# Attention and Silu FFN on one core: output weights by column halves, shorter segments, decay tables moved to GpSimd

## The chip, the core and the metric

The kernel runs on one core of a Trainium2 chip. The core has a matrix engine (TensorE, PE in the profile, its weight loads PEld), three engines for elementwise work (VectorE or DVE, ScalarE or ACT, GpSimd or POOL), and SyncE (SP), which here only issues transfers. Engines run on their own and wait for each other through semaphores. Matrix results land in PSUM and must be copied out ("evicted") by VectorE or ScalarE. Transfers between HBM and the on-chip SBUF are issued by SyncE or GpSimd and carried by 16 DMA engines.

The metric is device time in microseconds (us), the median of the timed executions.

## The reference

Four sequences of 768 positions, eight heads of 64. A linear attention with decay runs over blocks of 64 positions and carries a 64x64 state per head; its output goes through a two-layer FFN with Silu.

```python
for b in range(nb):                       # nb = 12 blocks
    qb, kb, vb = (q[:, :, sl], k[:, :, sl], v[:, :, sl])
    intra = np.einsum('bhic,bhjc->bhij', qb, kb) * Dmask[None]
    intra = np.einsum('bhij,bhjd->bhid', intra, vb)
    inter = np.einsum('bhid,bhde->bhie', qb * lam_pow[None], kv_state)
    out[:, :, sl] = intra + inter
    kb_dec = kb * rev_pow[None]
    kv_state = lam_block[None, :, None, None] * kv_state + np.einsum('bhsd,bhse->bhde', kb_dec, vb)
# ... x = out, heads side by side: 3072 x 512
h = x @ w_in                              # 512 x 2048
g = h * (1.0 / (1.0 + np.exp(-h)))        # Silu
return (g @ w_out)                        # 2048 x 512, result 3072 x 512
```

## The kernel before

Everything is written as small operations with priorities. A planner inside the kernel, which runs while the program is built, gives each a place on an engine. The order on every engine is fixed by that; at run time only semaphores decide when an operation starts.

The 3072 rows are 24 chunks of 128 (two blocks each). Chunks are gathered into groups for the FFN. The names in the profile: `h` is a PSUM tile of FFN1 (also used for transposes), `g` its Silu, `o` the PSUM tile of FFN2, `ob` the result. `big` is a pool of three 1 MB staging buffers, shared by w_in, w_out and v.

```python
GROUPS = [2, 2, 2, 2, 2, 2, 4, 4, 4]      # chunks in each FFN group
NHALF = 0                                 # groups whose FFN2 runs in two column halves
VP = 3                                    # the first VP segments have v issued by SyncE, the others by GpSimd
ORDER = "k0 q0 v0 k1 v1 wi0 wi1 q2 k2 v2 k3 v3 wi2 wi3 G:v3 S0 wo0 wo1 wo2 wo3 G:wo2 S1 S2 S3 S4 S5 S6"
SEGS = [(0, 8, 4), (1, 0, 4), (1, 4, 8), (2, 0, 6), (2, 6, 6), (3, 0, 6), (3, 6, 6)]   # sequence, first block, blocks
```

ORDER is the order in which loads are issued: k, q and v of the first four chunks, w_in and w_out in four pieces each, then segments S0 to S6, which bring k, q and v of the other chunks. `G:v3` is a gate: GpSimd waits there until v3 has landed. A segment's k comes in eight transfers (one per head) from GpSimd, cast on the way; its v in eight transfers as well.

A weight piece is loaded into `big` and cast to bf16 in two halves, by VectorE or ScalarE:

```python
def load_w(which, i, cast=False):
    if which == "in":
        src, dst = w_in_r[:, :, 512 * i:512 * i + 512], w_in_bf[:, :, 512 * i:512 * i + 512]
    else:
        src, dst = w_out_r[:, 4 * i:4 * i + 4, :], w_out_bf[:, 4 * i:4 * i + 4, :]
    # ... (a casting load, unused here)
    nc.sync.dma_start(out=t.tile, in_=src)                  # t: a buffer of big
    # ... for j in range(2): d, r are halves of dst and t.tile
        nc.scalar.activation(d, r, AF.Copy)                 # or
        nc.vector.tensor_copy(d, r)
        # ... wdep[which, m] = this cast, for the row blocks m that it brings
```

The FFN of a group. FFN2 sums over 16 row blocks of w_out, so the last of its matmuls needs the last piece:

```python
def ffn1(g, m0):
    # ...
            for ko in range(4):
                nc.tensor.matmul(hb.tile[:, i, :], lhsT=w_in_bf[:, ko, m * 128:(m + 1) * 128], rhs=xt[g].tile[:, ko, :], ...)
    # ...
        nc.scalar.activation(gb.tile, hb.tile..., AF.Silu)

def ffn2(g, mt):
    parts = 2 if g < NHALF else 1
    w = DM // parts
    for part in range(parts):
        # ...
        for kk in range(4):
            # ... for m in range(4 * kk, 4 * kk + 4):
                    nc.tensor.matmul(po.tile, lhsT=gt.tile[...], rhs=w_out_bf[:, m, cs], start=(m == 0), stop=(m == 15))
            deps += [wdep["out", m] for m in ms]
        # ... eviction of po to ob by VectorE or ScalarE, then two output transfers
```

The decay factors of the positions are six tables in `tabo`. The first is an exponential; the other five are the first times a power of lambda per head pair, made by ScalarE in four operations each. VectorE multiplies the attention's output by its table to give x. The buffers that hold k of a segment are zeroed by VectorE before their first use:

```python
zk = [const.tile([128, 8, NP, 2, D], BF16, name=f"kseg{i}") for i in range(3)]
o_zk = [[add(lambda t=t, i=i: nc.vector.memset(t[:, i], 0.0), ("DVE", 280.0), prio=-20.0 + 5.0 * n) for i in range(8)]
        for n, t in enumerate(zk)]
# ...
for i in range(1, NB):                    # NB = 6
    o_tabs.append([add(lambda i=i, p=p: nc.scalar.activation(
        tabo[:, p, i * C:i * C + C], tabo[:, p, 0:C], AF.Copy, scale=tab[:, 76 + 4 * i + p:77 + 4 * i + p]),
        ("ACT", 300.0), prio=TPR[i], at=TAT[i], deps=o_tabs[0]) for p in range(NP)])
```

ScalarE holds the tables of its functions in sets, and a set must be loaded before a function of it runs. The kernel asks for the set with exponential and logarithm at its start; the load for Silu is placed ahead of the first Silu. While TensorE has nothing to do in the first 26 us of the plan, it multiplies zeros (`zt`, L845).

Of the kernel before, what the change touches and what calls it, by code (L numbers as in the profile page):

```python
# [7 lines left out]
F32 = mybir.dt.float32  # L8
BF16 = mybir.dt.bfloat16
# [3 lines left out]

GROUPS = [2, 2, 2, 2, 2, 2, 4, 4, 4]
NHEAD = 4
NHALF = 0
NPET = 12
NPETQ = 16
WARM = 26000.0
VP = 3  # L20
ORDER = "k0 q0 v0 k1 v1 wi0 wi1 q2 k2 v2 k3 v3 wi2 wi3 G:v3 S0 wo0 wo1 wo2 wo3 G:wo2 S1 S2 S3 S4 S5 S6"
SEGS = [(0, 8, 4), (1, 0, 4), (1, 4, 8), (2, 0, 6), (2, 6, 6), (3, 0, 6), (3, 6, 6)]


class Op:
# [23 lines left out]
LATE = 60000.0  # L49
BIAS = 100.0  # L50
BIAS2 = 0.0
ZP = [[-150.0, -65.0, -64.0], [-140.0, -63.0, -50.0], -61.5]
TAT = [0.0, 10000.0, 17000.0, 19000.0, 30000.0, 31000.0]
TPR = [-90.0, -44.0, -43.0, -42.0, -22.0, -21.0]


# [114 lines left out]
def kernel(  # L171
# [20 lines left out]
    psum = ctx.enter_context(tc.tile_pool(name="psum", bufs=1, space=bass.MemoryType.PSUM))  # L192
    ctx.enter_context(tc.manual_schedule())

    SLOTS = {"qf": 3, "qb": 3, "qT": 4, "big": 3, "kbh": 2, "kfh": 2, "vfh": 3, "kseg": 3, "kT": 4, "vs": 3, "vbd": 3,
             "ss": 3, "sbd": 3, "x": 3, "g": 24, "ob": 5, "sc": 1, "op": 1, "kv": 1, "h": 3, "o": 2}
    PS = {"sc", "op", "kv", "h", "o"}

# [37 lines left out]


    zkh = [const.tile([128, 2, NP, 2, D], BF16, name=f"kbh{i}") for i in range(SLOTS["kbh"])]
    zk = [const.tile([128, 8, NP, 2, D], BF16, name=f"kseg{i}") for i in range(SLOTS["kseg"])]
    zv = [const.tile([128, 2, NP, 2, D], BF16, name=f"vbd{i}") for i in range(SLOTS["vbd"])]  # L240
    zs = [const.tile([128, NP, 2, D], BF16, name=f"sbd{i}") for i in range(SLOTS["sbd"])]
    nc.vector.memset(zkh[0], 0.0)
# [84 lines left out]
    def load_kh(c, eng, cast=False):  # L327
        if cast:
            t, os = Buf("kbh"), []
            r = k[0, :, C * c:C * c + C, :].rearrange("(p two) (s t) d -> two t s p d", two=2, t=2)  # L330
            for h in range(2):
                for s in range(2):
                    def f(h=h, s=s):
                        t.tile = zkh[t.idx % SLOTS["kbh"]]
                        hs = slice(64 * h, 64 * h + 64)
                        nc.gpsimd.dma_start(out=t.tile[hs, s, :, h, :], in_=r[h, s])
                    os.append(load(f, 65536, 128.0, 256, eng="POOL", alloc=[] if os else [t], uses=[t] if os else []))
            return t, os, None, None
        t, tf = Buf("kbh"), Buf("kfh")
        r = k[0, :, C * c:C * c + C, :].rearrange("(p two) (s t) d -> two s p (t d)", two=2, t=2)  # L340
        os = []
        for h in range(2):
            hs = slice(64 * h, 64 * h + 64)

            def f(h=h, hs=hs):
                if h == 0:
                    new(tf, [128, NP, 2, D], F32)
                QS[eng].dma_start(out=tf.tile[hs].rearrange("a p s d -> a p (s d)"), in_=r[h])
            o = load(f, 131072, 225.0, 256, eng=eng, alloc=[] if h else [tf], uses=[tf] if h else [])

            def fc(e, h=h, hs=hs):
                if h == 0:
                    t.tile = zkh[t.idx % SLOTS["kbh"]]
                dst, src = t.tile[hs, :, :, h], tf.tile[hs].rearrange("a p s d -> a s p d")
                if e == "ACT":
                    nc.scalar.activation(dst, src, AF.Copy)
                else:
                    nc.vector.tensor_copy(dst, src)
            os.append(add(fc, [("DVE", 420.0), ("ACT", 500.0)], deps=[o], alloc=[] if h else [t],
                          uses=[tf] + ([t] if h else []), after=os[-1:], prio=c - 62))  # L360
            if t.idx < 2 and h == 0:
                os[-1].deps += o_zkh[t.idx]
        return t, os, tf, o
# [14 lines left out]
    def load_kseg(b, c0, n):  # L378
        t = Buf("kseg")
        os = []  # L380
        for hh in range(H):
            def f(hh=hh):
                p, two = divmod(hh, 2)
                t.tile = zk[t.idx % SLOTS["kseg"]]
                hs = slice(64 * two, 64 * two + 64)
                nc.gpsimd.dma_start(out=t.tile[hs, 0:n, p, two, :],  # L386
                                    in_=k[b, hh, 64 * c0:64 * (c0 + n), :].rearrange("(c s) d -> s c d", s=64))
            os.append(load(f, 16384 * n, 128.0, 64 * n, eng="POOL", alloc=[] if hh else [t], uses=[t] if hh else [],
                           deps=o_zk[t.idx] if t.idx < SLOTS["kseg"] else []))
        return t, os  # L390

    def load_vseg(b, c0, n, eng):
# [12 lines left out]

    wdep, wlast = {}, {}

    def load_w(which, i, cast=False):

        if which == "in":  # L410
            src, dst = w_in_r[:, :, 512 * i:512 * i + 512], w_in_bf[:, :, 512 * i:512 * i + 512]
        else:
            src, dst = w_out_r[:, 4 * i:4 * i + 4, :], w_out_bf[:, 4 * i:4 * i + 4, :]
        if cast:
            o = load(lambda: nc.gpsimd.dma_start(out=dst, in_=src), 1048576, 312.0, 512, eng="POOL")
            for m in range(4 * i, 4 * i + 4):
                wdep[which, m] = o
            return

        t = Buf("big")  # L420

        def f():
            new(t, [128, 4, 512], F32)
            nc.sync.dma_start(out=t.tile, in_=src)
        o = load(f, 1048576, 370.0, 512, alloc=[t], issue=450.0)
        wlast[which, i] = (t, o)
        for j in range(2):
            def fc(e, j=j):
                if which == "in":
                    d, r = dst[:, :, 256 * j:256 * j + 256], t.tile[:, :, 256 * j:256 * j + 256]  # L430
                else:
                    d, r = dst[:, 2 * j:2 * j + 2, :], t.tile[:, 2 * j:2 * j + 2, :]
                if e == "ACT":
                    nc.scalar.activation(d, r, AF.Copy)  # L434
                else:
                    nc.vector.tensor_copy(d, r)
            z = add(fc, [("DVE", 750.0), ("ACT", act_ns(1024, True))], deps=[o], uses=[t], prio=-20 + 0.1 * i)
            for m in range(4 * i + 2 * j, 4 * i + 2 * j + 2):
                wdep[which, m] = z

    gt_ = const.tile([128, 16], F32, name="gt_")
    ngate = [0]
# [284 lines left out]
    def ffn2(g, mt):  # L727
# [4 lines left out]
        for part in range(parts):  # L732
# [3 lines left out]
            for kk in range(4):  # L736
                ms = range(4 * kk, 4 * kk + 4)

                def f(kk=kk, ms=ms, po=po, cs=cs):
                    if kk == 0:  # L740
                        new(po, [128, w], F32, padded=[128, DM])
                    for m in ms:
                        gt, _, g0 = gts[g, m]
                        nc.tensor.matmul(po.tile, lhsT=gt.tile[:, g0 + mt * C:g0 + (mt + 1) * C], rhs=w_out_bf[:, m, cs],  # L744
                                         start=(m == 0), stop=(m == 15))
                deps = [gts[g, m][1] for m in ms] + ([prev] if prev else [])
                deps += [wdep["out", m] for m in ms]
                prev = add(f, ("PE", pe_ns(4, w)), deps=deps, alloc=[po] if kk == 0 else [],
                           uses=([] if kk == 0 else [po]) + list({id(gts[g, m][0]): gts[g, m][0] for m in ms}.values()),
                           prio=PF + 100 * g + 20 + 4 * mt + kk + (8 if part else 0))  # L750
# [20 lines left out]
    def zero(t, cols, first, prio):  # L771
        if first:
# [5 lines left out]
    o_zs = [zero(t, 512, i == 0, ZP[0][i]) for i, t in enumerate(zs)]  # L778
    o_zv = [zero(t, 1024, i < 2, ZP[1][i]) for i, t in enumerate(zv)]
    o_zkh = [[], zero(zkh[1], 1024, True, ZP[2])]  # L780
    o_zk = [[add(lambda t=t, i=i: nc.vector.memset(t[:, i], 0.0), ("DVE", 280.0), prio=-20.0 + 5.0 * n) for i in range(8)]
            for n, t in enumerate(zk)]
    o_iota = add(c_iota, ("POOL", 1000.0), prio=-200)
    chain["POOL"].append(o_iota)
    o_id = add(c_ident, ("DVE", 300.0), prio=-199, deps=[o_iota])
# [2 lines left out]
    o_tab = add(c_tab, ("ACT", 1700.0), at=3400.0, prio=-100, deps=[o_id])  # L788
    o_tabs = [[add(lambda p=p: nc.scalar.activation(tabo[:, p, 0:C], io, AF.Exp, scale=lla[:, p:p + 1]), ("ACT", 300.0),
                   prio=-90, deps=[o_tab]) for p in range(NP)]]  # L790
    for i in range(1, NB):
        o_tabs.append([add(lambda i=i, p=p: nc.scalar.activation(  # L792
            tabo[:, p, i * C:i * C + C], tabo[:, p, 0:C], AF.Copy, scale=tab[:, 76 + 4 * i + p:77 + 4 * i + p]),
            ("ACT", 300.0), prio=TPR[i], at=TAT[i], deps=o_tabs[0]) for p in range(NP)])

    def seg(i):
        b, c0, n = SEGS[i]
# [9 lines left out]
    for item in ORDER.split():  # L807
# [8 lines left out]
        elif item[0] == "q":  # L816
            landed[item] = load_q(int(item[1]), "POOL" if item[2:] == "p" else "SP")
        elif item[0] == "w":
            which = "in" if item[1] == "i" else "out"
            load_w(which, int(item[2]), item[3:] == "c")  # L820
            landed[item] = wlast.get((which, int(item[2])))
        elif item[0] == "S":
            seg(int(item[1]))
        else:
            buf, dep = landed[item[2:]]
            gate(buf, dep)
# [56 lines left out]
```

## Time and profile before

| | |
|---|---|
| time, median of 3 | 226.24 us (225.97 to 226.25) |
| span of the profiled execution | 225.2 us |
| TensorE busy | 212.4 us (94%), 1898 matmuls |
| ScalarE busy | 124.9 us (55%) |
| VectorE busy | 108.5 us (48%) |
| GpSimd busy | 68.9 us (31%) |
| warm-up matmuls on zt | 82 |
| HBM read, written | 27.27 MB, 6.29 MB |

The page's second part cuts the span into 40 slices of 5.6 us and gives the busy tenths of each engine in each; its row PEclk is the clock granted to TensorE. The table of stages gives busy time between two points in time. The chain of waits goes back from the last instruction, at each step to what released it; a line is a start, a length and the work. A busy TensorE need not be doing useful work, and matmuls overlap: the mean duration of one is longer than the distance from one to the next, so prices are taken from runs of equal matmuls in the chain.

### The profile page before, as it was taken

What the parts mean: (1) busy time and instruction counts of PE and PEld (TensorE: products, weight loads), DVE (VectorE), ACT (ScalarE), POOL (GpSimd) and SP (SyncE); (2) the same over time, 40 slices, a digit from 0 to 9 for tenths busy, and PEclk for the clock granted to TensorE, in tenths of its full rate; (3) what the DMA queues carried; (4) which work ended last, traced back from release to release, by engine and by line L of the source; (5) the groups of instructions that cost most, each with busy time, mean ns of one, the idle gap of its engine ahead of it and who ended that gap; (6) DMA issues with size and microseconds to landing.
All of it is one profiled execution on the core that took longest, in us unless ns stands there. A gap on an engine that the chain in (4) does not pass through costs nothing.

```text
span 225.2 us, 4817 instructions
## 1 busy us (share of the span) xinstructions
PE 212.4 (94%) x1898; PEld 136.6 (61%) x1922; DVE 108.5 (48%) x244; ACT 124.9 (55%) x236; POOL 68.9 (31%) x111
## 2 busy tenths in 40 slices
PE   6996999799999999999999999999999999999991
PEld 4785888666488487879578554555455444444440
DVE  7987696364476527897358255363644100000000
ACT  6799899765185276556338346741375512555211
POOL 2000910086635499887736470000000000000000
PEclk9999699999999999999999999999999999999999
DMA  4999999689999988999999999395220013300052
GB/s 126 264 361 234 374 191 345 214 260 194 228 215 272 160 194 178 159 194 222 205 129 237 156 173 163 92 153 107 67 50 0 3 29 76 82 0 3 0 125 62
DMA packets 64485, 35.44 MB, mean 157 GB/s; under 512 B 48848, under 2 KB 54992, under 8 KB 64464
## 3 DMA queue, kind: packets, MB, share of 16 engines
q1 hardware_dynamic: 39968, 24.13, 49.7%
q0 software_dynamic: 24352, 11.02, 34.8%
q8 instruction: 15, 0.25, 0.5%
q14 instruction: 6, 0.05, 0.1%
q10 hardware_dynamic: 144, 0.00, 0.0%
HBM read 27.27 MB, written 6.29 MB: 149 GB/s over the span
## 4 chain that ended last, share of the span: by engine, by line
PE 80%; ACT 12%; DMA 4%; issue 1%; SPq 1%; DVE 1%; ACTq 0%
PE o L744 34%; PE h L712 34%; PE op L644 4%; DMA qf<-in_q_dram 2%; ACT w_in_bf L434 2%; PE h L516 2%; ACT g L720 2%; PE kv L664 2%; PE sc L616 2%; ACT tabo L792 2%; ACT sbd L676 1%; PE h L480 1%; ACT vbd L559 1%; DMA out_dram<-ob 1%; ACT w_out_bf L434 1%
## 5 line engine op out<-in xcount | busy, mean ns | idle before, releaser
L712 PE MATMUL h<-x,w_in_bf 128*128 128x256 bf16 (+1 forms) x569 | 90.5, 309 | 1.4 <-ACT w_in_bf L434 0.5
L744 PE MATMUL o<-w_out_bf,g 128*128 128x512 bf16 x367 | 86.3, 379 | 2.3 <-ACT w_out_bf L434 1.4
L720 ACT ACTIVATE g<-h 128x512 bf16<-128x512 f32 x96 | 57.2, 597 | 30.2 <-PE h L712 29.7
L712 PEld LDWEIGHTS <-w_in_bf 128*128 128x128 bf16 x576 | 54.7, 99 | 27.2 <-ACT w_in_bf L434 1.4
L744 PEld LDWEIGHTS <-g 128*128 128x128 bf16 x384 | 36.0, 98 | 39.8 <-issue 1.7
L386 POOL DMA_DIRECT2D kseg<-in_k_dram x56 | 37.3, 690 | 18.4 <-DMA qf<-in_q_dram 14.6
L756 ACT ACTIVATE ob<-o 128x512 f32<-128x512 f32 x24 | 14.3, 598 | 49.5 <-PE o L744 38.6
L678 DVE CAST sbd<-kv 64x256 bf16<-64x256 f32 x40 | 16.9, 421 | 20.5 <-PE kv L664 16.6
L401 POOL DMA_DIRECT2D big<-in_v_dram x32 | 21.1, 671 | 8.3 <-DMA kseg<-in_k_dram 4.6
L691 DVE TENSOR_TENSOR x<-op,tabo 128x512 bf16<-128x512 f32 x24 | 16.5, 689 | 9.7 <-PE op L644 8.7
L676 ACT ACTIVATE sbd<-kv 64x256 bf16<-64x256 f32 x40 | 15.0, 376 | 10.6 <-PE kv L664 10.1
L622 DVE TENSOR_TENSOR ss<-sc,mask 128x512 bf16<-128x512 f32 x20 | 13.8, 688 | 11.6 <-PE sc L616 11.6
L644 PE MATMUL op<-ss,vbd 128*128 128x64 bf16 (+1 forms) x192 | 16.3, 197 | 0.0
L644 PE MATMUL op<-qT,sbd 128*128 128x64 bf16 (+1 forms) x160 | 15.0, 195 | 0.0
L845 PE MATMUL sc<-zt 128*128 128x256 bf16 x82 | 13.6, 318 | 1.1 <-DVE zt L228 1.1
L561 DVE COPY vbd<-vs 64x512 bf16<-64x512 bf16 x44 | 14.0, 318 | 0.5
L644 PEld LDWEIGHTS <-vbd 128*128 128x128 bf16 x192 | 12.6, 98 | 1.7 <-ACT vbd L559 0.3
L550 DVE TENSOR_TENSOR vs<-big,tab 128x512 bf16<-128x512 f32 x20 | 13.1, 685 | 0.9 <-DMA big<-in_v_dram 0.8
L523 DVE COPY kT<-h 128x1024 bf16<-128x1024 bf16 x9 | 6.0, 686 | 14.6 <-PE h L516 14.6
L644 PEld LDWEIGHTS <-sbd 128*128 128x128 bf16 x160 | 11.6, 98 | 1.4
L845 PEld LDWEIGHTS <-zt 128*128 128x128 bf16 x82 | 8.9, 114 | 2.7 <-DVE zt L228 1.1
L310 POOL DMA_DIRECT2D qf<-in_q_dram x10 | 9.1, 912 | 4.4 <-ACT g L720 1.7
(58 smaller groups left out, 144.7 us busy)
## 6 DMA issues: line engine op xcount, KB each, us to landing
out_dram<-ob SPq DMA_DIRECT2D x48, 128.0 KB, 3.4
qf<-in_q_dram POOLq DMA_DIRECT2D x10, 512.0 KB, 8.4
big<-in_moe_w_in_dram SPq DMA_DIRECT2D x4, 1024.0 KB, 7.8
big<-in_moe_w_out_dram SPq DMA_DIRECT2D x4, 1024.0 KB, 6.2
big<-in_v_dram POOLq DMA_DIRECT2D x32, 96.0 KB, 5.9
kseg<-in_k_dram POOLq DMA_DIRECT2D x32, 48.0 KB, 7.0
kfh<-in_k_dram SPq DMA_DIRECT2D x8, 128.0 KB, 5.4
qf<-in_q_dram SPq DMA_DIRECT2D x2, 512.0 KB, 8.2
```

What stands on the lines that cost most here:

```text
L386: nc.gpsimd.dma_start(out=t.tile[hs, 0:n, p, two, :], in_=k[b, hh, 64 * c0:64 * (c0 + n), :].rearrange("(c s) d -> s c d", s=64))
L401: QS[eng].dma_start(out=t.tile[hs, :, p, :], in_=v[b, hh, 64 * c0:64 * (c0 + n), :].rearrange("(c s) d -> s c d", s=64))
L561: nc.vector.tensor_copy(vb.tile[hs, :, :, h, :], tv.tile[hs])
L644: nc.tensor.matmul(o_cols(p, sub), lhsT=l, rhs=r, start=not ovs["started"], stop=i == len(steps) - 1, skip_group_check=True)
L676: nc.scalar.activation(nb.tile[hs, :, h, :], kvp.tile[hs], AF.Copy)
L678: nc.vector.tensor_copy(nb.tile[hs, :, h, :], kvp.tile[hs])
L691: nc.vector.tensor_tensor(xt[g].tile[:, :, C * off:C * off + C], ob.tile, tabo[:, :, C * blk:C * blk + C], op=AL.mult)
L712: nc.tensor.matmul(hb.tile[:, i, :], lhsT=w_in_bf[:, ko, m * 128:(m + 1) * 128], rhs=xt[g].tile[:, ko, :], start=(ko == 0), stop=(ko == 3) ...
L720: nc.scalar.activation(gb.tile, hb.tile.rearrange("a i n -> a (i n)"), AF.Silu)
L744: nc.tensor.matmul(po.tile, lhsT=gt.tile[:, g0 + mt * C:g0 + (mt + 1) * C], rhs=w_out_bf[:, m, cs], start=(m == 0), stop=(m == 15))
L756: nc.scalar.activation(bo.tile[:, cs], po.tile, AF.Copy)
L845: nc.tensor.matmul(zp, lhsT=zt[:, 0:128], rhs=zt, start=nz == 0, stop=True, skip_group_check=True)
```

## The change

Four things are changed together.

- w_out is loaded in pieces of eight row blocks by 256 columns instead of four row blocks by 512. The first two groups compute FFN2 in column halves (NHALF = 2), so that the left half needs only the first two pieces. The order of the loads is changed to bring these ahead of the first segment S0, which is gated by the third piece of w_in.
- All segments are of four blocks; there are ten instead of seven, with five smaller buffers for k instead of three. Only the first segment's v is issued by SyncE.
- The tables 2 to 5 are made by GpSimd, one operation each; table 1 stays on ScalarE. The zeroing of the later k buffers is put off.
- Silu's table set is asked for right after the first decay table.

They are meant to let the FFN start earlier and to relieve ScalarE and VectorE at the start.

```diff
-NHALF = 0
+NHALF = 2
-VP = 3
-ORDER = "k0 q0 v0 k1 v1 wi0 wi1 q2 k2 v2 k3 v3 wi2 wi3 G:v3 S0 wo0 wo1 wo2 wo3 G:wo2 S1 S2 S3 S4 S5 S6"
-SEGS = [(0, 8, 4), (1, 0, 4), (1, 4, 8), (2, 0, 6), (2, 6, 6), (3, 0, 6), (3, 6, 6)]
+VP = 1
+ORDER = "k0 q0 v0 k1 v1 wi0 wi1 q2 k2 v2 k3 v3 wi2 wi3 wo0 wo1 G:wi2 S0 wo2 wo3 G:wo2 S1 S2 S3 S4 S5 S6 S7 S8 S9"
+SEGS = [(0, 8, 4)] + [(b, c, 4) for b in range(1, 4) for c in (0, 4, 8)]
...
+TPOOL = (2, 3, 4, 5)
+ZAT = [0.0, 34000.0, 38000.0, 45000.0, 50000.0, 55000.0]
-TAT = [0.0, 10000.0, 17000.0, 19000.0, 30000.0, 31000.0]
+TAT = [0.0, 10000.0, 0.0, 0.0, 0.0, 0.0]
...                                        # SLOTS: kseg 3 -> 5
-    zk = [const.tile([128, 8, NP, 2, D], BF16, name=f"kseg{i}") ...
+    zk = [const.tile([128, 4, NP, 2, D], BF16, name=f"kseg{i}") ...
...                                        # load_w
-            src, dst = w_out_r[:, 4 * i:4 * i + 4, :], w_out_bf[:, 4 * i:4 * i + 4, :]
+            r0, cs = 8 * (i % 2), slice(256 * (i // 2), 256 * (i // 2) + 256)
+            src, dst = w_out_r[:, r0:r0 + 8, cs], w_out_bf[:, r0:r0 + 8, cs]
...                                        # ffn2
-                deps += [wdep["out", m] for m in ms]
+                deps += [wdep["out", m, hf] for m in ms for hf in ((part,) if parts == 2 else (0, 1))]
...
-    o_zk = [[add(lambda t=t, i=i: nc.vector.memset(t[:, i], 0.0), ..., prio=-20.0 + 5.0 * n) for i in range(8)]
+    o_zk = [[add(lambda t=t, i=i: nc.vector.memset(t[:, i], 0.0), ..., prio=-20.0 + 5.0 * n, at=ZAT[n])
+             for i in range(4)] for n, t in enumerate(zk)]
...
+    add(lambda: nc.scalar.preload_act_table_set("silu_and_others"), ("ACT", 1290.0), prio=-89, after=o_tabs[0])
+
+    def scaled(i, p=None):
+        if p is None:
+            nc.gpsimd.tensor_tensor(tabo[:, :, i * C:i * C + C], tabo[:, :, 0:C],
+                                    tab[:, 76 + 4 * i:80 + 4 * i, None].to_broadcast([128, NP, C]), op=AL.mult)
+        else:
+            nc.scalar.activation(tabo[:, p, i * C:i * C + C], tabo[:, p, 0:C], AF.Copy, scale=...)
     for i in range(1, NB):
-        o_tabs.append([... nc.scalar.activation(...) for p in range(NP)])
+        if i in TPOOL:
+            o_tabs.append([add(lambda i=i: scaled(i), ("POOL", 1150.0), ...)])
+        else:
+            o_tabs.append([add(lambda i=i, p=p: scaled(i, p), ("ACT", 300.0), ...) for p in range(NP)])
```

## The prediction

> **What bounds the kernel now.** I read the page's slices first. The TensorE row (PE) is full from slice 9 on; ScalarE (ACT) is full in slices 2 to 7, where TensorE is not.
>
> ```profile
> PE   6996999799999999999999999999999999999991
> ACT  6799899765185276556338346741375512555211
> PEclk9999699999999999999999999999999999999999
> ```
>
> Then the busy time by stage, cut where the chain of waits changes character (columns: the stage, its length, busy time of PE, PEld, DVE, ACT, POOL, granted clock, DMA share, GB/s).
>
> ```profile
> 17.17:22.27 5.10, 3.25 (x29) 2.59 (x30) 3.51 (x11) 5.07 (x8) 0.03 (x1) 1.00 1.00 225
> 22.27:30.44 8.17, 7.68 (x90) 6.72 (x89) 5.96 (x15) 7.35 (x16) 5.46 (x9) 0.79 1.12 330
> 30.44:37.57 7.13, 6.72 (x68) 5.88 (x69) 5.13 (x15) 7.06 (x15) 0.61 (x1) 1.00 1.28 255
> 37.57:44.60 7.03, 5.62 (x49) 4.89 (x50) 3.83 (x9) 5.86 (x13) 0.00 (x0) 1.00 0.78 270
> 44.60:217.00 172.40, 171.18 (x1510) 103.42 (x1532) 75.39 (x154) 84.78 (x156) 61.58 (x90) 1.00 0.84 134
> ```
>
> After 44.60 us TensorE has no gaps worth naming. Is that busy time work? The chain gives the price of a matmul: eight of 256 columns take 0.87 us (109 ns each), four of 512 take 0.86 (216), eight of 64 take 0.23 (29), eight of 128 take 0.45 (57). With these prices the program's useful matmuls (the warm-up ones on zt left out) come to 198.4 us: FFN1 41.9 + 41.5, FFN2 82.9, attention and transposes 32. In the program's order, 22.6 us of them stand before the point where the chain resumes at 44.60, so 175.8 are left; the last one ends at 220.1, 175.5 later. The steady part is therefore packed, and the rest of the span is two pieces: 44.6 - 22.6 = 22.0 us lost in the head, and 5.1 us after the last matmul (an eviction of 0.6 and an output transfer). At 17.17 only 3.9 us of the useful work is done, so of the 22.0 some 13.3 are lost before 17.17, waiting for the first loads, and 8.7 between 17.17 and 44.60.
>
> The chain of waits says on what. The lines below are from its part between 16 and 45 us (start, length, what):
>
> ```profile
> 16.17 2.84 ACT w_in_bf L434 x3
> 19.01 0.29 ACT tabo L792
> ...
> 19.32 1.28 ACT L720
> 20.61 0.60 ACT g L720
> ...
> 28.57 0.87 ACT tabo L792 x3
> 29.44 0.56 ACT w_in_bf L434
> ...
> 37.57 5.42 PE h L712 x48
> ...
> 43.01 0.60 ACT g L720
> 43.61 0.95 ACT w_out_bf L434
> ```
>
> ScalarE is the chain here: casts of w_in, decay tables, a table load (L720 with no tile), evictions through Silu. Only after 37.57 does TensorE lead, and at 42.8 to 44.6 it waits for a w_out cast, whose load was late. By the transfers' view the third w_in chunk is issued at 19.7 and lands 5.6 us later, at 25.3; ScalarE casts it at 29.34. So that chunk waits four us for an engine, not for the DMA.
>
> **What the Trainium skill says.** "ScalarE: Activation LUTs", What ACT_TABLE_LOAD costs: 1283 ns for any set. The trace agrees, 1283 ns in both rows. "TensorE: Matmul & The Clock Gate", Back-to-back issue gap: warm matmuls follow each other at N/2.4 + 2.5 ns, so halving N from 512 to 256 adds about 2.5 ns a pair; the trace agrees (216 against 2 x 109). "GPSIMD Engine Reference", Elementwise: a two-input fp32 operation takes about 2.6 cycles an element at 1.2 GHz. A table of 512 elements is then an estimated 1.1 to 1.3 us; no run here shows one yet. "SBUF — State Buffer", Who interferes with whom: GpSimd and two-port VectorE operations exclude each other for an instruction. The trace of before has no such pair to test it with in the head.
>
> **The change, part by part.**
>
> *Silu's table early.* The load of 1.28 us stands at 19.32 in the chain. It moves to just behind the first decay table, near 6.0. There ScalarE idles 1.46 us before its first cast of q, on that transfer. Hidden: 1.3 us off the ScalarE chain.
>
> *Tables on GpSimd.* Of 20 small activations that scale a table, 16 leave ScalarE. They cost 0.29 to 0.31 each when they follow each other (three in 0.87). Between 16 and 37.6, 15 or so run, and 4 of the 20 stay on ScalarE before 16; taken off in this stretch: about 15 x 0.30 = 4.5 us. GpSimd gets four operations, an estimated 4.6 to 5.2 us, behind the first table at 6 us; it is idle until 22.2 there. The second pair's x needs its table near 29. Hidden.
>
> *VectorE zeroing.* The 24 zeroings of kseg (272 ns) all lie before 35 us in the kernel before. Now there are 20, 4 in the head and 16 from 34 us on, so VectorE gains 5 us in the head. Two of the three between 8.23 and 9.05, which are on the chain ahead of the qT copy, go: 0.5 us. The new instruction order uses the freed time: VectorE takes 4 of the 8 w_in casts instead of 2, which lifts 2 x 0.95 = 1.9 us off ScalarE.
>
> ScalarE thus sheds 1.3 + 4.5 + 1.9 = 7.7 us in the stretch whose chain it is. TensorE cannot follow by all of that, since other things come next: the loads. The third w_in chunk still lands at about 25, the fourth came at 29.3 with S0's q, k and v beside it. In the new order these wait for the third chunk or stand behind two w_out chunks, so I put the fourth at 28. Where TensorE reached useful work 16.7 (chain: 36.57 us), it still owes after the fourth pair's attention (k3 and v3 land at 22.2, then some 4 us of copies, scores, mask) 3.5 us of FFN1: 27.5 + 3.5 = 31, with a stall of 1 to 2 for the first w_out half about 32.5. I take 4 us saved up to here.
>
> *w_out by halves.* Before, the first w_out load is issued at 32.16 and lands at 38.2, since it stands behind S0's v and waits for a free buffer; the last lands at 50.4. Now the first stands directly behind w_in, issued at about 21 and landed near 31. Two loads bring all 16 row blocks of columns 0 to 255, enough for 64 half-width matmuls (7.0 us of TensorE) of the first two groups. This replaces the gaps of 0.39 and 1.41 at 37.2 and 43.2: 1.8 us, of which I count 1.2. Its price: 64 more matmuls, 64 x 2.5 ns = 0.16 us, and four more evictions, off the path.
>
> *Segments of four blocks.* This makes nothing faster by itself. GpSimd issues go from 98 to 162 (9 segments of q, 8 k, 8 v, and one of q and k). A segment's 17 issues take 0.91 + 16 x 0.67 = 11.6 us, and the 61.6 us busy in the 90 us to 135 show that waits add to it. TensorE spends on a segment's two pairs 2 x (6.9 of FFN + 1.3 of attention) = 16.4 us. GpSimd is faster, but from a gate near 42 us the first segments have by my count only about 2 us in hand. I take 0.5 us of new stalls.
>
> Sum: -4.0 - 1.2 + 0.2 + 0.5 = -4.5, and 0.3 for the earlier start at 8 to 9 us: -4.8. Prediction 226.24 - 4.8 = 221.4 us. The span's end, 5.1 us, stays.
>
> **Rivals.** *The DMA takes over the head.* The same 11 MB have to land, and the transfers already run at 225 to 330 GB/s there. For it: DMA shares of 1.0 to 1.3. If the fourth w_in chunk and the first w_out stay near 30 and 36, ScalarE's free time turns into waiting and only 2 us come: 224. Against: the third chunk waits four us after landing. *GpSimd becomes the bound.* With 162 issues, v on its queue and 8 transfers in flight at most, segments come late, and a static order makes each late segment a TensorE gap. For it: POOL waits 14.6 us on q transfers now. Against: 16.4 against 11.6. It would cost 2 to 5 us: 223 to 227. *The whole head is recovered.* If TensorE is fed from 28 us on without stalls, and the slow clock (0.79 in 22 to 30) goes too, up to 7.5 of the 8.7 us return: 218.5.
>
> **Range and chances.** Second and third rivals bound it: 217.8 to 225.8. The 2% line is 221.7, so close to the middle that it decides: the ScalarE slack is solid, the landings are not. Faster by over 2%: 0.54; within: 0.41; slower: 0.05.
>
> **What would show it.** The table load and its 1.28 us gone from the chain and standing near 6 us; the POOL tables at about 1.2 us each before 15 us; ScalarE no longer full in 17 to 37; the w_in casts within a us or two of landing; the first FFN2 matmul near 32 instead of 42.8; and TensorE packed after about 40 with no longer gaps named by kseg, big or kT. I am wrong if the head's chain turns to "DMA big", if the first FFN2 stays after 38, or if gaps of over 2 us in sum appear after 50.

## The result, and the profile after

| | before | after |
|---|---|---|
| time, median (range) | 226.11 us (225.47 to 226.25) | 224.39 us (223.66 to 228.01) |
| ratio, 95% interval | | 0.992 (0.989 to 0.995) |
| span of the profiled execution | 225.2 us | 223.8 us |
| TensorE, VectorE, ScalarE, GpSimd busy | 94, 48, 55, 31% | 95, 52, 52, 49% |

The change gains 1.7 us where 4.8 were predicted. The profile used for "after" is that of run a_again, the same kernel once more, since in the first execution one transpose of k landed only after 16.6 us and TensorE waited 1.6 us for it.

The rows of slices of a_again, for the engines whose work moved:

```profile
PE   6699999999999999999999999999999999999991
ACT  6857977767465365647264166631555611555211
POOL 2700281059959999979999594989000000000000
PEclk9769999999999999999999999999999999999999
```

ScalarE is less full in slices 3, 4, 6 and 7 than it was (5, 7, 7 and 7 tenths, all 9 before), and GpSimd works nearly through slices 9 to 28, as ten segments want. TensorE looks fuller in the head, but this is deceptive. The stages of a_again, with the same columns as before the change, and the third and fourth cut at its first FFN2 matmul:

```profile
17.17:22.27 5.10, 5.10 (x58) 4.64 (x55) 4.42 (x10) 3.99 (x6) 0.00 (x0) 1.00 0.95 181
22.27:30.44 8.17, 8.03 (x109) 7.15 (x107) 7.02 (x15) 7.15 (x12) 3.87 (x6) 1.00 0.99 352
30.44:36.00 5.56, 5.20 (x52) 4.58 (x52) 2.70 (x6) 3.87 (x6) 2.48 (x5) 1.00 1.26 278
36.00:44.60 8.60, 8.60 (x83) 7.75 (x83) 3.68 (x11) 6.37 (x13) 0.16 (x1) 1.00 1.02 189
44.60:217.00 172.40, 171.19 (x1559) 107.95 (x1578) 84.30 (x181) 83.04 (x146) 97.19 (x154) 1.00 0.75 137
```

In 17.17 to 22.27 TensorE is busy all the time, against 3.25 of 5.10 before. Much of that multiplies zeros: the chain below has 1.53 and 1.20 us of L858, the warm-up. In 30.44 to 36.00 only 5.20 of 5.56 us are busy. VectorE works 2.70 us of that stage and ScalarE 3.87, so neither is full. The wide stage to 217 is as packed as it was (171.19 busy, 171.18 before), though GpSimd works 36 us more in it and VectorE 9.

The chain of waits of a_again in the head:

```profile
17.29 1.53 PE sc L858 x14
18.82 0.67 PE op L644 x12
19.49 1.20 PE sc L858 x11
20.69 1.75 PE h L712 x16
...
25.95 0.60 ACT g L720
26.55 0.51 ACT vbd L559
27.07 0.63 ACT vbd L559
27.70 0.02 issue
27.73 1.02 ACT kT L521
28.75 0.02 issue
28.77 1.07 ACT w_in_bf L430
29.86 0.04 issue
29.91 10.34 DMA big<-in_moe_w_out_dram
```

The table load (L720 without a tile) and the tables are gone from it, as predicted. What stands there is, first, a chain of copies on ScalarE for the fourth chunk, and then the transfer of the second w_out piece, issued at 29.9 and landed at 40.2. The chain of a run whose tables are on ScalarE (a_tables_act) tells the last part more plainly, since it follows the first w_out piece to the first FFN2 matmul:

```profile
21.80 13.37 DMA big<-in_moe_w_out_dram
35.20 0.70 DVE w_out_bf L432
35.90 0.04 issue
35.94 1.91 PE o L744 x16
```

The piece is issued at 21.8, as the prediction said, and lands at 35.2, 13.4 us later.

To count what was lost I take, as the prediction did, the position of a matmul less the useful matmul time ahead of it in the program's order (its prices of 109, 216, 57 and 29 ns; 198.4 us in all, 198.5 with the halves):

| | first FFN1 | first FFN2 | useful before it | lost | last matmul | lost |
|---|---|---|---|---|---|---|
| before | 17.2 | 42.8 | 22.4 | 20.4 | 220.1 | 21.7 |
| a_again | 20.5 | 36.0 | 16.7 | 19.3 | 219.0 | 20.5 |
| a_again_2 | 20.7 | 35.8 | 16.7 | 19.1 | 218.9 | 20.3 |
| a_tables_act | 19.4 | 35.9 | 16.7 | 19.2 | 219.0 | 20.5 |
| a_half_wout | 18.4 | 35.0 | 16.7 | 18.2 | 218.0 | 19.5 |
| a_gate_wo0 | 18.4 | 33.7 | 16.7 | 17.0 | 220.7 | 22.2 |
| b_silu_again | 18.3 | 41.6 | 22.4 | 19.2 | 218.0 | 19.6 |
| b_halves | 16.9 | 37.4 | 15.8 | 21.5 | 226.1 | 27.6 |
| b_segs | 16.8 | 42.7 | 22.4 | 20.2 | 228.9 | 30.5 |

The first FFN2 matmul stands 6.8 us earlier, but 5.7 us of useful work that stood before it now stands behind it. What TensorE loses in all falls by 1.2 us, and the tail after the last matmul from 5.1 to 4.8.

### The profile page after: what moved, and what is told of

It is laid out like the page before. It is cut to its first block, busy times and chain, and to the rows that moved or that the text cites. A ratio compares the mean times of both kernels' runs of the same rounds, so it can differ in the third digit from the quotient of the medians.

```text
span 226.2 us, 5035 instructions
## 1 busy us (share of the span) xinstructions
PE 212.7 (94%) x1968; PEld 141.8 (63%) x1988; DVE 115.9 (51%) x258; ACT 116.7 (52%) x206; POOL 109.3 (48%) x179
## 3 DMA queue, kind: packets, MB, share of 16 engines
q0 software_dynamic: 25504, 12.59, 40.2%
## 4 chain that ended last, share of the span: by engine, by line
PE 71%; DMA 20%; SPq 3%; ACT 3%; issue 1%; DVE 1%; ACTq 0%; DVEq 0%
PE o L744 31%; PE h L712 30%; DMA kT<-kseg 7%; DMA big<-in_moe_w_out_dram 6%; DMA qf<-in_q_dram 5%; PE op L644 3%; PE sc L616 2%; PE kv L664 2%; PE h L516 2%; PE h L480 1%; SPq L351 1%; SPq L377 1%; DMA out_dram<-ob 1%; ACT g L720 1%; ACT ob L756 1%
## 5 line engine op out<-in xcount | busy, mean ns | idle before, releaser
L744 PE MATMUL o<-w_out_bf,g 128*128 128x512 bf16 (+1 forms) x435 | 88.9, 348 | 2.0 <-DVE w_out_bf L432 1.2
L720 ACT ACTIVATE g<-h 128x512 bf16<-128x512 f32 x96 | 56.6, 595 | 34.7 <-PE h L712 32.6
L712 PEld LDWEIGHTS <-w_in_bf 128*128 128x128 bf16 x576 | 54.0, 98 | 24.8 <-issue 0.4
L744 PEld LDWEIGHTS <-g 128*128 128x128 bf16 x448 | 41.7, 98 | 34.2 <-issue 1.6
L389 POOL DMA_DIRECT2D kseg<-in_k_dram x80 | 50.1, 678 | 23.2 <-DMA qf<-in_q_dram 15.3
L404 POOL DMA_DIRECT2D big<-in_v_dram x72 | 44.6, 640 | 2.7 <-DMA kseg<-in_k_dram 1.5
L756 ACT ACTIVATE ob<-o 128x512 f32<-128x512 f32 (+1 forms) x26 | 14.2, 547 | 50.0 <-PE o L744 37.9
L678 DVE CAST sbd<-kv 64x256 bf16<-64x256 f32 x62 | 26.1, 422 | 23.7 <-PE kv L664 20.9
L691 DVE TENSOR_TENSOR x<-op,tabo 128x512 bf16<-128x512 f32 x24 | 16.6, 691 | 8.6 <-PE op L644 8.2
L858 PE MATMUL sc<-zt 128*128 128x256 bf16 x84 | 13.4, 313 | 1.1 <-DVE zt L231 1.1
L664 PEld LDWEIGHTS <-kseg 128*128 128x128 bf16 x144 | 8.9, 98 | 5.0 <-issue 0.3
L322 ACT ACTIVATE qb<-qf 128x512 bf16<-128x512 f32 x14 | 8.6, 624 | 5.4 <-DMA qf<-in_q_dram 5.4
L858 PEld LDWEIGHTS <-zt 128*128 128x128 bf16 x84 | 8.9, 111 | 2.7 <-DVE zt L231 1.1
```

The source lines that it names most:

```text
L389: nc.gpsimd.dma_start(out=t.tile[hs, 0:n, p, two, :], in_=k[b, hh, 64 * c0:64 * (c0 + n), :].rearrange("(c s) d -> s c d", s=64))
L404: QS[eng].dma_start(out=t.tile[hs, :, p, :], in_=v[b, hh, 64 * c0:64 * (c0 + n), :].rearrange("(c s) d -> s c d", s=64))
L678: nc.vector.tensor_copy(nb.tile[hs, :, h, :], kvp.tile[hs])
L691: nc.vector.tensor_tensor(xt[g].tile[:, :, C * off:C * off + C], ob.tile, tabo[:, :, C * blk:C * blk + C], op=AL.mult)
L720: nc.scalar.activation(gb.tile, hb.tile.rearrange("a i n -> a (i n)"), AF.Silu)
L756: nc.scalar.activation(bo.tile[:, cs], po.tile, AF.Copy)
```

## The experiments

A name with a_ is the changed kernel with an edit, one with b_ the kernel before with an edit. Every ratio is to the kernel before. Spans are of one execution and scatter by about 1 us between executions of one kernel (222.2 and 223.0 for the same text below), so the ratios decide.

**a_again, a_again_2: the changed kernel, no edit.**

> The changed kernel once more, for a second profile: the first one shows a DMA transpose of k landing after 16.6 us near 120 to 137 us. If that wait is part of the change (late segments), it is there again and the span is near 226; if it is a chance of that execution, it is gone and the span is near 222.5. Under both, the first w_out cast stays near 35.5 us and the two casts of q on VectorE stay near 1 us each.

> The changed kernel, beside the last on the same chip: ratio 0.990 to 0.994 as before.

Measured: 0.9924 (0.9899 to 0.9948) and 0.9924 (0.9887 to 0.9961). The gain is 0.76%, 1.7 us, each time. The first FFN2 stands at 36.0 and 35.8. In a_again_2 the first w_out piece lands two us earlier than in a_again, at 33.2, and its cast begins at once. VectorE and TensorE of a_again_2:

```profile
33.20 0.69 DVE L432 CAST w_out_bf<-big 128x1024 bf16<-128x1024 f32 x1
...
35.79 1.91 PE L744 MATMUL o<-w_out_bf,g 128*128 128x256 bf16 x16
```

FFN2 comes only 0.2 us sooner for it: TensorE goes from FFN1 to FFN2 without a wait, so in this execution the landing of w_out held nothing up.

**a_tables_act: the tables back on ScalarE.**

```diff
-TPOOL = (2, 3, 4, 5)
-TAT = [0.0, 10000.0, 0.0, 0.0, 0.0, 0.0]
+TPOOL = ()
+TAT = [0.0, 10000.0, 17000.0, 19000.0, 30000.0, 31000.0]
```

> The changed kernel with the tables 2 to 5 back on ScalarE. Theory 1 (the four table operations on GpSimd at 6.1 to 10.5 us hold up VectorE's casts of q, and the whole head shifts by 1.2 us): the casts take 0.43 us again, the first FFN1 starts near 17.2 instead of 18.4, third w_in piece lands near 25.3, and the time falls by 0.5 to 1.2 us, to about 223.4. Theory 2 (ScalarE's relief is what brings the gain): the time rises by 1 to 3 us, to 225.5 to 227.

Measured: 0.9917 (0.9886 to 0.9948), level with the changed kernel; together the two intervals could hide some 0.9 us. Why the tables' move isn't a clear gain is seen where the four GpSimd operations run. GpSimd of a_again:

```profile
6.14 4.40 POOL L795 TENSOR_TENSOR tabo<-tabo,tab 128x512 f32<-128x512 f32 x4 [4.11 <-ACT tabo L789]
```

VectorE of a_again beside it, from 7.5 us:

```profile
7.55 2.09 DVE L324 CAST qb<-qf 128x512 bf16<-128x512 f32 x2 [0.26 <-DMA qf<-in_q_dram]
...
10.12 0.97 DVE L550 TENSOR_TENSOR vs<-vfh,tab 128x512 bf16<-128x512 f32 x1
```

and the same two of a_tables_act, where GpSimd does nothing at that time:

```profile
8.71 0.76 DVE L324 CAST qb<-qf 128x512 bf16<-128x512 f32 x2 [1.08 <-DMA qf<-in_q_dram]
...
10.19 0.68 DVE L550 TENSOR_TENSOR vs<-vfh,tab 128x512 bf16<-128x512 f32 x1
```

Two casts of q take 2.09 us instead of 0.76, and a multiply 0.97 instead of 0.68. The operations on GpSimd take the 1.1 us each that were estimated, but they are not hidden: they slow VectorE by 1.6 us, 1.3 of it ahead of the first copy of qT. What ScalarE gains and what VectorE loses both stand in the level result; no run takes them apart.

**b_halves, b_segs, b_relief: one part each, on the kernel before.**

b_halves takes the column halves of w_out with the new order of loads, and leaves segments, tables and Silu's table as they were:

```diff
-NHALF = 0
+NHALF = 2
-... wi2 wi3 G:v3 S0 wo0 wo1 wo2 wo3 G:wo2 S1 ...
+... wi2 wi3 wo0 wo1 G:wi2 S0 wo2 wo3 G:wo2 S1 ...
+            r0, cs = 8 * (i % 2), slice(256 * (i // 2), 256 * (i // 2) + 256)   # and the casts and waits by halves
```

> The kernel before with w_out by column halves and the new place of w_out in the order of loads alone; segments, tables and Silu's load as before. If the halves and the order carry the gain: 224 to 225. If ScalarE bounds the head (the prediction's reading), its chain hides the earlier w_out, and the time stays at 225.5 to 226.5. First w_out cast near 36 if the DMA is the limit, near 32 if not.

Measured: 1.0246 (1.0194 to 1.0298), slower by 1.9 to 3.0%. Its first FFN2 comes at 37.4, but the time is given back later. A stage of b_halves near 100 us:

```profile
95.00:110.00 15.00, 11.42 (x151) 9.22 (x150) 13.41 (x30) 6.09 (x11) 7.43 (x12) 0.89 1.21 223
```

TensorE idles 3.6 of 15 us there, its clock falls to 0.89, and VectorE is the full engine. Two of TensorE's waits in it:

```profile
98.03 0.28 PE L664 MATMUL kv<-vs,kseg 128*128 128x64 bf16 x4 [1.10 <-DVE sbd L678]
...
101.31 0.34 PE L664 MATMUL kv<-vs,kseg 128*128 128x64 bf16 x4 [1.64 <-DVE sbd L678]
```

These matmuls belong to attention. Between the last FFN2 matmuls, at 94.5 to 96.1, and the next FFN1 run at 102.9 TensorE has no FFN work to fill such waits with: two chunks' attention, block by block through VectorE, must be done before there is any. GpSimd of b_halves also waits 14.5 us, in two waits, for one of its three large k buffers to come free of these matmuls; whether that is a cause or a consequence was not tried. In a_again 93 to 110 us is full (16.84 of 17).

b_segs takes the ten segments and the five smaller buffers, and nothing else:

```diff
-VP = 3
-SEGS = [(0, 8, 4), (1, 0, 4), (1, 4, 8), (2, 0, 6), (2, 6, 6), (3, 0, 6), (3, 6, 6)]
+VP = 1
+SEGS = [(0, 8, 4)] + [(b, c, 4) for b in range(1, 4) for c in (0, 4, 8)]   # kseg: 5 buffers of 4 blocks; ORDER goes on to S9
```

> The kernel before with ten segments of four blocks, five k buffers, v of all but S0 issued by GpSimd; w_out, tables and Silu's load as before. If short segments only prevent a shortage that the earlier w_out makes: 226 to 227.5, no gain. If they help by themselves (fewer bytes ahead of need, VectorE zeroing 20 instead of 24): 224.5 to 225.5.

Measured: 1.0343 (1.0267 to 1.0419), slower. GpSimd's waits in b_segs (total, times, longest):

```profile
POOL kseg L386 <- DMA qf<-in_q_dram: 18.9, 8, 5.2
```

and in a_again:

```profile
POOL kseg L389 <- DMA qf<-in_q_dram: 5.0, 3, 3.1
```

Its segments arrive late: the last one's q lands at 163.6 us, against 150.8 in a_again. Those waits alone don't explain it, since the kernel before has 14.6 us of them with fewer and larger segments. TensorE of b_segs pays:

```profile
131.00 0.28 PE L664 MATMUL kv<-vs,kseg 128*128 128x64 bf16 x4 [1.54 <-DVE sbd L678]
...
165.72 0.19 PE L644 MATMUL op<-ss,vbd 128*128 128x64 bf16 x1 [2.10 <-DVE ss L622]
```

Neither large part is a gain alone. Why GpSimd waits less in the whole change was not tried separately.

b_relief takes the other two, the early Silu table and the tables on GpSimd:

```diff
+TPOOL = (2, 3, 4, 5)                       # scaled() on GpSimd as in the changed kernel
+TAT = [0.0, 10000.0, 0.0, 0.0, 0.0, 0.0]
+    add(lambda: nc.scalar.preload_act_table_set("silu_and_others"), ("ACT", 1290.0), prio=-89, after=o_tabs[0])
```

> The kernel before with Silu's table loaded early and the tables 2 to 5 on GpSimd, nothing else: ScalarE relieved by some 6 us in the head. The prediction's reading (ScalarE's time is the head's time until 37.6): FFN1 of the first two groups ends 3 to 4 us earlier and the time falls by 2 us or more, to 224 or less, unless w_out's landing takes over. Rival (the loads bound the head, ScalarE's work was slack filled in): FFN1 ends at most 1 us earlier, the first FFN2 waits for w_out, and the time stays within 0.7 us of before.

Measured: 0.9946 (0.9927 to 0.9964), 1.2 us. VectorE of b_relief shows the same slow casts of q, 1.97 us for two.

**a_norelief: the changed kernel without those two.** The early Silu table is taken out and the tables are on ScalarE, so it has halves and segments together (and the later zeroing).

> The changed kernel without its two reliefs of ScalarE: tables back on ScalarE and Silu's table loaded where it was; that leaves the column halves and the segments of four. Alone on the kernel before, halves cost 2.5% and segments 3.4%. If each needs the other (the earlier w_out uses the FFN work up, short segments bring attention in time), this is level with the changed kernel or at most 0.5% behind it, ratio 0.992 to 0.998 to before. If the two just add up and the reliefs save them, it is 3 to 6% slower than before.

Measured: 0.9975 (0.9952 to 0.9997). Alone the parts cost 2.5% and 3.4%; together they gain a quarter of a per cent. So they pay only in company. That company has the later zeroing in it, which neither b_halves nor b_segs has; its share was not tried. The step from here to the changed kernel, half a per cent, is about what the early Silu table brings alone (below).

**b_silu, b_silu_again: the early Silu table alone.**

```diff
+    add(lambda: nc.scalar.preload_act_table_set("silu_and_others"), ("ACT", 1290.0), prio=-89, after=o_tabs[0])
```

> The kernel before with Silu's table loaded early and nothing else: 1.28 us off ScalarE in the stretch where it is the chain. By the prediction 1.0 to 1.3 us faster (ratio 0.994 to 0.9955). If the chunk chain (theory 3) sets the head, 0.5 us or less.

> The kernel before with Silu's table loaded early, once more, since its first interval (0.9845 to 0.9929) is wide. If the early load alone is worth more than the whole change: ratio 0.985 to 0.991 again, last matmul near 217.3 us. If the first time was a lucky one: 0.993 or more.

Measured: 0.9887 (0.9845 to 0.9929), and with more executions 0.9940 (0.9917 to 0.9963): 1.4 to 2.6 us from one line. ScalarE of b_silu:

```profile
6.06 1.28 ACT L791 ACT_TABLE_LOAD   x1
```

The 1.28 us now lie where ScalarE would wait for q, and not at 19.32. This alone is worth about what the whole change is, and b_relief, which adds the tables on GpSimd to it, is not ahead of it.

**a_gate_wo0: S0's transfers held until the first w_out piece has landed.**

```diff
-... wo0 wo1 G:wi2 S0 ...
+... wo0 wo1 G:wo0 S0 ...
```

> The changed kernel with the loads of segment S0 on GpSimd held until the first w_out piece has landed, not the third w_in piece. If the DMA bandwidth of 22 to 36 us is the limit, the fourth w_in piece lands near 28.5 instead of 30.5 and the first w_out piece near 32.5 instead of 35.5, FFN2 starts about 2 to 3 us earlier, and the time falls by 1 to 2 us unless S0 then comes too late near 47 us. If those pieces wait for anything else (a staging buffer, a slot of the queue), they land as before and the time stays or rises.

Measured: 0.9974 (0.9952 to 0.9996), half a per cent behind a_again. The first w_out piece lands at 32.1, three us earlier, so S0's traffic did delay it. The run of 32 FFN1 matmuls behind the fourth chunk starts earlier too (30.25, against 32.09 in a_again), and FFN2 follows without a wait:

```profile
30.25 3.66 PE L712 MATMUL h<-x,w_in_bf 128*128 128x256 bf16 x32
33.74 1.91 PE L744 MATMUL o<-w_out_bf,g 128*128 128x256 bf16 x16
```

So 2.3 us are won here. The first FFN1 is earlier too, at 18.4, before the gate can matter; but the first execution of the changed kernel also had it at 18.4, and its first FFN2 came at 36.3. The 2.3 us are lost again, and more, when S0 is late. Two later stages of a_gate_wo0:

```profile
45.00:55.00 10.00, 8.58 (x124) 7.82 (x122) 6.30 (x14) 6.71 (x14) 9.42 (x15) 1.00 0.94 168
55.00:65.00 10.00, 9.00 (x121) 8.13 (x119) 5.75 (x12) 5.04 (x10) 8.75 (x14) 1.00 0.99 207
```

TensorE idles 2.4 us in these 20; a_again has 9.86 and 9.97 busy in the same two.

**a_half_wout, b_half_wout: half the bytes of w_out.** Of each piece only the first half of the row blocks is transferred and used twice. Both kernels leave out half of w_out, so their outputs aren't the reference's; the instructions stay the same.

```diff
-            nc.sync.dma_start(out=t.tile, in_=src)
+            nc.sync.dma_start(out=t.tile[:, 0:4], in_=src[:, 0:4])     # w_out only; before: 0:2
...                                        # both casts of a piece read these rows
```

> The changed kernel with half of each w_out piece left out of the transfer (four of eight row blocks are loaded, and used twice), so 2 MB less come in the first 45 us; the order on all engines is the same. Theory 1 (the bytes of the head bound the changed kernel): the first w_out piece lands 2 us or more earlier (33.5 or before instead of 35.3), S0's loads land earlier too, the gaps near 47 to 54 go, and the time falls by 1.5 to 3 us to 221.5 to 223. Theory 2 (engines and the fixed order bound the head): under 0.7 us.

> The kernel before with half of each w_out piece left out of the transfer in the same way, same order on all engines. Its head is, by the chain, ScalarE's until 37.6 us and its w_out comes late in the order of issue, so theory 1 and 2 both expect little up to 42.8 us; the gap of 1.4 us at 43 to 44.6 is a ScalarE cast after Silu evictions, so it stays as well. Time within 1 us of before. A fall of 2 us or more would say that before too was bound by bytes.

Measured: 0.9922 (0.9892 to 0.9952) for the changed kernel, no different from whole pieces, and 0.9995 (0.9975 to 1.0014) on the kernel before. TensorE of a_half_wout:

```profile
31.46 3.66 PE L713 MATMUL h<-x,w_in_bf 128*128 128x256 bf16 x32
34.96 1.91 PE L745 MATMUL o<-w_out_bf,g 128*128 128x256 bf16 x16
```

and the cast of its first piece on VectorE:

```profile
32.34 0.68 DVE L433 CAST w_out_bf<-big 128x1024 bf16<-128x1024 f32 x1
```

w_out is ready 2 us before TensorE is, and FFN2 comes only 1 us earlier than in a_again: right behind the landing stands a second limit, TensorE's own way through the fourth chunk. In the times this 1 us doesn't show; the two intervals together could hide some 0.9 us.

**a_q2_first, a_q2_first_act: the loads of the second pair moved up,** to bring that second limit forward; the second with the tables on ScalarE.

```diff
-... v1 wi0 wi1 q2 k2 v2 k3 v3 wi2 ...
+... v1 wi0 q2 k2 v2 wi1 k3 v3 wi2 ...
```

> The changed kernel with the second q and the third chunk's k and v loaded ahead of the second w_in piece, and the fourth chunk's k and v behind it. Theory 3 (what sets the head is the attention of chunks 2 and 3, whose loads land at 20.6 to 23 us and which then needs some 8 us through the engines one after the other): q2 lands near 17.5 instead of 20.3, the fourth chunk's scores and the FFN1 run behind them start at 29 to 30 instead of 31.4, and the time falls by 1 us or more, to ratio 0.988 or less. If w_in's landing sets it (fourth piece at 30.5 in both), the time stays within 0.3%.

> The same order of loads with the tables on ScalarE, so that VectorE's first casts of q aren't held up by GpSimd. With theory 3 the first FFN1 comes 1 us earlier than in the changed kernel and the whole is the fastest of this study, ratio 0.982 to 0.988. If ScalarE's time counts, it is behind the same order with the tables on GpSimd.

Measured: 0.9935 (0.9908 to 0.9963) and 0.9945 (0.9923 to 0.9968), no gain. This doesn't settle whether the loads of q2 and k2 set the second limit, for the edit moves other loads back: in a_q2_first q2 lands at 16.8 (20.2 in a_again), but k3 at 24.1 (22.6), the fourth w_in piece at 31.5 (29.7) and the first w_out piece at 36.2 (35.2). TensorE of a_q2_first meets another wait instead:

```profile
29.58 1.05 PE L712 MATMUL h<-x,w_in_bf 128*128 128x256 bf16 x8 [1.19 <-ACT w_in_bf L430]
```

**Four attempts at a better version.** b_silu_t45_zat is b_silu with two tables and two thirds of the zeroing put off beyond the head. a_act_t45 is a_tables_act with tables 4 and 5 at 37 and 38 us of the plan. a_act_eights is a_tables_act with the half-width FFN2 in runs of eight matmuls instead of four, meant to fill the waits between attention steps near 50 us. a_best has both.

```diff
+TAT = [0.0, 10000.0, 17000.0, 19000.0, 37000.0, 38000.0]               # b_silu_t45_zat, a_act_t45, a_best
+... prio=-20.0 + 5.0 * n, at=(0.0, 33000.0, 38000.0)[n])               # b_silu_t45_zat
+        nk = 4 // parts                                                 # a_act_eights, a_best
+        for kk in range(nk):
+            ms = range(16 // nk * kk, 16 // nk * kk + 16 // nk)
```

> The same with the tables 4 and 5 (8 operations of 0.3 us, still on ScalarE) put off to 37 us, and the zeroing of the second and third k buffer put off to 33 and 38 us on VectorE. If fillers on ScalarE and VectorE between 20 and 37 us hold up the chunk chain: 1 us faster than with the early load alone, ratio near 0.984. If they only fill gaps: level with it.

> The changed kernel with the tables on ScalarE, 4 and 5 put off to 37 us. If ScalarE still counts in the head of the changed kernel: 0.7 us or more faster than with the tables early (0.9917). If w_out's landing at 35.3 us has taken over: level, 0.990 to 0.993.

> The changed kernel with the tables on ScalarE, and the half-width FFN2 cut into runs of eight matmuls (0.87 us) instead of four (0.44 us). If the gaps of some 1 us in sum between 45 and 55 us come from filler between dependent attention steps that became half as long, they go, and it is 0.7 us or more faster than the variant with fours (ratio 0.9885 or less, against 0.9917). If the w_out and S0 loads make them, it is level or slower, since a run of eight needs both its pieces at once.

> The changed kernel with the tables on ScalarE, 4 and 5 put off, and the half-width FFN2 in runs of eight. If the two small gains add (each some 0.3% against the changed kernel): ratio 0.983 to 0.987. If both only remove the same wait for the first w_out piece: 0.988 to 0.990, level with each alone.

Measured: 0.9906 (0.9872 to 0.9940), 0.9880 (0.9847 to 0.9912), 0.9889 (0.9857 to 0.9922), 0.9887 (0.9844 to 0.9930). The last three lie some 0.4% ahead of the changed kernel, with overlapping intervals, and don't add up. For a_act_eights the mechanism meant is not the one seen. TensorE of a_act_eights still waits near 50 us:

```profile
49.94 0.28 PE L664 MATMUL kv<-vs,kseg 128*128 128x64 bf16 x4 [1.04 <-DVE sbd L678]
```

Its first FFN2 is earlier (34.9, 17.3 us lost), as the planner placed more FFN1 work ahead of it. For a_act_t45 the trace shows the same wait for w_out (1.66 us before the first FFN2) and no cause for a gain.

## Why the prediction was wrong, step by step

**What bounds the kernel.** Right as a reading: the steady part is packed, what can be won lies in the head, and ScalarE was its chain. The 7.7 us are too many: between 16 and 37.6 us the trace of before has 12 of the table operations that leave ScalarE, not 15, so 3.6 us, and ScalarE's busy time in that stretch fell from 20.64 to 17.30 us. And beside ScalarE's chain ran a second one, through the fourth chunk, that I didn't follow (below).

**Silu's table, 1.3 us.** Right, and the only term that held by itself: alone it brings 1.4 to 2.6 us. "TensorE cannot follow by all of that" proved truer than I made it.

**Tables on GpSimd, "Hidden".** The price was right (1.10 us each), the word was not. I had read the Trainium skill's "SBUF — State Buffer", Who interferes with whom, and found no pair in the head of the old trace to test it with; the new kernel makes one, and the trace agrees with the page: 2.09 us for two casts instead of 0.76. After that loss the ScalarE time set free (my 4.5 us) leaves nothing that the times show: a_tables_act, with neither, is level.

**The failed step: 4 us saved up to the first FFN2.** It rests on three sentences: "I put the fourth at 28", "issued at about 21 and landed near 31" and "some 4 us of copies, scores, mask". At equal useful work TensorE stands at 36.00 instead of 36.57: 0.6 us saved, not 4. The runs show two limits close to each other in its place.

1. *The landing.* In three profiles of the changed kernel (the first execution, a_again, a_again_2) the fourth w_in piece landed at 30.5, 29.7 and 28.1 and the first w_out piece at 35.5, 35.2 and 33.2. By a_gate_wo0, S0's own q and k are what shares the DMA with it: held back, the piece lands at 32.1. I had counted the queue ahead of it on SyncE, and not what GpSimd issues beside it. TensorE waits 1.2, 0.25 and 0 us for the piece in the three profiles, and 1.6 to 1.7 in a_tables_act and a_act_t45.
2. *TensorE's readiness.* In a_again_2 the fourth w_in piece came when I had put it, at 28, and w_out before TensorE could use it, and the first FFN2 stands at 35.8 all the same. FFN1 behind the fourth chunk ends only at 33.7 to 35.8 in the variants of this kernel, where I had 31. From k3's last cast to the end of the fourth chunk's mask are 6.5 us in a_again, and to the end of its x 8.5, where I had 4 (and even 22.2 and 4 don't make my 27.5). The old trace had it already. VectorE of before:

```profile
24.08 0.41 DVE L358 CAST kbh<-kfh 64x512 bf16<-64x512 f32 x1
...
32.68 0.68 DVE L691 TENSOR_TENSOR x<-op,tabo 128x512 bf16<-128x512 f32 x1
```

This x ends at 33.4 in before, at 33.1 in a_again, at 32.1 in the first execution and at 31.6 in a_tables_act: the relief of ScalarE moved it by 0.3 to 1.7 us. VectorE of a_again, from its last cast of k3 on:

```profile
24.60 0.42 DVE L361 CAST kbh<-kfh 64x512 bf16<-64x512 f32 x1
...
27.60 0.86 DVE L678 CAST sbd<-kv 64x256 bf16<-64x256 f32 x2 [0.34 <-PE kv L664]
28.49 0.69 DVE L432 CAST w_in_bf<-big 128x1024 bf16<-128x1024 f32 x1
29.21 0.69 DVE L691 TENSOR_TENSOR x<-op,tabo 128x512 bf16<-128x512 f32 x1
29.82 1.28 DVE L606 TENSOR_TENSOR ss<-h,mask 128x512 bf16<-128x512 f32 x2
31.02 0.68 DVE L432 CAST w_in_bf<-big 128x1024 bf16<-128x1024 f32 x1
32.37 0.69 DVE L691 TENSOR_TENSOR x<-op,tabo 128x512 bf16<-128x512 f32 x1 [0.67 <-PE op L644]
```

Between cast and mask stand state copies, a w_in cast and another chunk's x; on ScalarE the copy of kT waits behind two copies of vbd (26.55 to 27.73 in the chain above). I had summed the operations of this chunk and left out those that the fixed order puts between them. Easing the landing alone (a_half_wout) gave 1 us in its trace and nothing that the times show.

**Halves, 1.2 us.** Half right: the gaps at 37.2 and 43.2 are gone. After the point of 16.7 us of useful work TensorE lost 1.85 us before and loses 1.2 now, so 0.65 came. With the 0.6 above this is the 1.2 us of TensorE; the tail gives 0.3. The price of 2.5 ns a pair was right: sixteen matmuls of 256 columns take 1.75 us in a_again, 109 ns each. But the Trainium skill's "TensorE: Matmul & The Clock Gate", Back-to-back issue gap, gives N/2.4 + 2.5 ns for an isolated matmul and about 131 ns for 512 columns in a sustained stream; the 216 ns of this stream agree with the first figure and not with the second.

**Segments, 0.5 us of stalls.** For the whole change this was too careful: the long stage is as packed as before. What I didn't see is that the halves without them lose 2.5% (b_halves).

**The rivals.** The first is what happened in its visible half: it named 30 and 36 for the landings and 224 us for the time, and my sign for it, a head's chain that turns to "DMA big", came. It is not the whole cause, as a_half_wout and a_again_2 show. The second may hold for b_segs; in the whole change GpSimd is busier (109.3 us, 68.9 before) without bounding. The third did not happen; the clock in 22 to 30 us did recover, to 1.00, without saving the time.

**Open.** How much of the 8.5 us is the fixed order, and how much would remain with every engine free, no run tells. The cause of the small gains of a_act_t45 and a_act_eights isn't settled either.

## What to carry to other kernels

When the slack of one engine is to be turned into time, follow the next two chains to their ends, landing and readiness, with everything that a fixed order puts between; what hides behind the first limit may stand only one us away, and the old trace may show it already. Read more than one profile of a kernel before naming a wait: here the same program waited for w_out in one execution and not in another. Count for a landing all transfers that fly at that time, from every queue. And try a change of several parts part by part: here one line brought what the whole brought, and two other parts that cost 2.5 and 3.4% alone cost nothing together.

## What the runs showed of the hardware

Beside GpSimd's fp32 multiplies two casts of q on VectorE took 2.09 us (a_again) instead of 0.76 (a_tables_act). The same program's first w_out piece landed 11.9 to 13.3 us after its issue in three executions, and 10.7 with S0's loads held back. A slow start need not show: in a_again the granted clock is 0.7 and 0.6 in the second and third slices (5.6 to 16.8 us) and the first FFN1 stands at 20.5 us, where the first execution, at 0.9 or more, has 18.4; the first FFN2 stands at 36.0 and 36.3, since in the latter it waits 1.2 us for w_out.
